# Attention, gated unit and soft mixture on one core: another spread of conversion and gated unit over the first eight pairs, and work of VectorE given to GpSimd and ScalarE

## The chip, the cores and the metric

One core of a Trainium2 chip runs the whole program. Times are device microseconds of one execution. The kernel before was run three times; its profile comes from one more execution.

## The reference

Three stages follow each other (numpy, shortened). The inputs q, k and phi are scaled by 8, so the exponentials are sharp.

```
# q, k, v: [4, 8, 1152, 64]
q_pool = q.reshape(B, H, S // 2, 2, D).mean(axis=3)          # 576 queries
scores = scale * q_pool @ k.T ; scores -= max(scores)
attn = exp(scores) / (sum + 1e-9) ; x = attn @ v               # -> [2304, 512]
g = x @ w_gate ; val = x @ w_val                               # [512, 1536] each
x = (g * sigmoid(g) * val) @ w_out                             # [1536, 512]
logits = x @ phi                                               # 32 slots
d = softmax of logits over the tokens ; slot_input = d.T @ x
slot_out[e] = relu(slot_input[e] @ w1[e]) @ w2[e]              # 8 experts
out = softmax of logits over the slots @ slot_out
```

## The kernel before, in words

The 32 heads are worked in 16 pairs (`steps`: batch b, pair p of 4). A pair has 21 units: nine of 128 keys by 512 queries for each of its two heads, and three that hold the remaining 64 queries of both. Operands are split into a high and a low half of 16 bits. A unit (`unit`, line 405) is two score matmuls into a bank (`st`), one exponential on ScalarE into P32 (line 419), and the difference P32 - PH (line 426) that gives the low half PL; PH is the upper 16 bits of P32 in place. The product with the values (`pv`, lines 457 to 459) follows three units later (LAG); P32 and PL have six buffers each (PB).

`DVE_PART` gives, for each pair, the share of the differences that VectorE does; GpSimd does the others, and a pair beyond the list has share 0. `F32_PART` gives the share of units that have no difference at all, because they multiply P32 itself with the values (lines 449 and 455).

`split_pair` (line 210) prepares the next pair while this one runs: it adds the two pooled queries (227), casts keys and queries (`kh`, `qh`, lines 230 and 232), takes their low halves (`ql` on VectorE, `kl` on GpSimd) and has SP's queue copy the halves to where the matmuls read them (lines 241 to 250). `cast` (line 179) puts a cast on ScalarE if its letter is in CASTS and the pair is one of the first eight, else on VectorE. `row_max` (line 315) finds the maxima of the next pair from kh and QD: 18 matmuls of 512 columns and nine of 128, each reduced on VectorE (329, 338); the maxima are joined (nm, 341), negated on ScalarE (mt, 310) and sent by a DMA from ScalarE's queue into row 64 of QH (347), for which the second score matmul (414) of every unit waits. The first pair's maxima (`row_max_first`) come from its own halves.

Weights are converted while pairs run. `prep` holds 36 items, for each of six slices of the gated unit two of `prep_wo` (613) and four of `prep_w` (647). Each loads 512 words a partition through SP's queue, has ScalarE work on both halves (600, 601) and VectorE join them (603). `prep_wo` then writes w_out's rows to HBM and multiplies them with phi on TensorE; `prep_w` casts on ScalarE (653) and takes the low half (655) on GpSimd, or on VectorE for three of the 24. Items come evenly from step PREP_BEG to step PREP_END (line 979). At the end of them three pieces of w_out are loaded.

The gated unit works in nine blocks of 256 tokens, each in six slices of 48 matmuls of 256 columns (`block_slice`, 671; its tanh is line 696). `moe_stream` (924) yields after every quarter of a slice, 31 times a block; a slice waits until its weights are converted, a block until its batch of four pairs is done. The loop at line 975 takes quanta from the stream so that from step 4 to step 16 the count grows evenly to 6.1 blocks. What is left runs after the last pair, then come the experts and the output.

Each engine's own order of instructions is planned by a scheduler from the order of the program, priorities and a timeline of its own; on the chip each engine then runs its list in order.

Of the kernel before, what the change touches and what calls it, by code (L numbers as in the profile page):

```python
# [29 lines left out]
HI_DVE, LO_PART = 0.0, 1.0  # L30
LD0, LDP = 1, 4
Y5E = 2
DVE_PART = [0.3, 0.3, 0.0, 0.3, 0.0, 0.3]
CAST_STEPS = 8
LO_DVE = 3
BAR = 2
# [9 lines left out]
MOE_LEAD = 6  # L46
PB, LAG = 6, 3
MOE_START = 4
N_MOE = 6.1
PREP_BEG, PREP_END = 1, 7  # L50
F32_PART = [0.17, 0.0, 0.17, 0.25, 0.33]
VRB = 2
HNB = 1
SUBS = ""
CASTS = "vqwxt"
OB = 4
AHEAD = 0
TXD = 1
# [6 lines left out]
def tile_pool_attention_glu_softmoe(  # L65
# [35 lines left out]
    def ps(tag, shape, dtype=F32, bufs=1, name=None):  # L101
        return psum.tile(shape, dtype, tag=tag, bufs=bufs, name=name or tag)
# [50 lines left out]
    steps = [(b, p) for b in range(B) for p in range(NP)]  # L153
# [14 lines left out]
    def load_pair(b, p):  # L168

        r = slice(D if (b, p) == steps[0] else 0, P)  # L170
        kr = at.tile([P, S], F32, tag="kraw", bufs=1, name=f"kr{b}_{p}")
        nc.sync.dma_start(out=kr[r], in_=kT[b, p, r])
        qr = at.tile([P, 2, SQ], F32, tag="qraw", bufs=1, name=f"qr{b}_{p}")
        nc.sync.dma_start(out=qr[r], in_=qT[b, p, r])
        vr = at.tile([P, 2, NCH, D + 1], F32, tag="vraw", bufs=VRB, name=f"vr{b}_{p}")
        nc.sync.dma_start(out=vr, in_=vP[b, p])
        raw[b, p] = (kr, qr, vr)

    def cast(what, b, p, dst, src):

        if b * NP + p < CAST_STEPS and what in CASTS:
            ins = nc.scalar.copy(dst, src)
# [174 lines left out]
    def later(n, fn):  # L357

        due.append((now[0] + n, fn))

    def tick(n=1):
        now[0] += n
        while True:
            run = [d for d in due if d[0] <= now[0]]
            if not run:
                return
            due.remove(run[0])
            run[0][1]()
# [18 lines left out]
    def maxima(n):  # L387
        while n_rm[0] < min(n, MX0 + MXP * (len(steps) - 1)):
            next(maxs)
            n_rm[0] += 1  # L390
# [3 lines left out]
    def of_step(parts, i):  # L394
        return parts[i] if i < len(parts) else 0.0

    def share(n, part):

        n[0] += part
        if n[0] >= 1.0:  # L400
            n[0] -= 1.0
            return True
        return False

    def unit(b, p, key, parts, n):
# [18 lines left out]
        PL = at.tile([P, QT], F16, tag="PL", bufs=PB, name=f"PL{b}_{p}_{key}")  # L424
        eng = nc.vector if share(n_dve, of_step(DVE_PART, b * NP + p)) else nc.gpsimd
        eng.tensor_tensor(out=PL[:, :o], in0=P32[:, :o], in1=PH[:, :o], op=ALU.subtract)  # L426
# [452 lines left out]
    def load(n, mark=None):  # L879
        key = order[n]  # L880
        ts = place(n, "_".join(map(str, key)))
        m = NQ // len(ts)

        piece[key] = [ts[e // m][:, e % m] for e in range(NQ)]
        for i, t in enumerate(ts):
            if key[0] == "w2":
                _, z, g, c = key
                k = HALF // ZW[z]
                t = t.rearrange("p e (c d) -> p e c d", c=k)
                for e in range(m):  # L890
                    src = w2[NQ * g + i * m + e, c * P:(c + k) * P, Z0[z]:Z0[z] + ZW[z]]
                    dma = nc.sync.dma_start(out=t[:, e], in_=src.rearrange("(c p) d -> p c d", p=P))
                    if mark and e >= Y5E:
                        after(dma, mark)
                continue
            if key[0] == "wo":
                src = wo_d[key[1] * NQ * P:(key[1] + 1) * NQ * P, :].rearrange("(c p) d -> p c d", p=P)
            else:
                e = slice(NQ * key[1] + i * m, NQ * key[1] + (i + 1) * m)
                src = w1[e, key[3] * P:(key[3] + 1) * P, key[2] * HALF:(key[2] + 1) * HALF]  # L900
                src = src.rearrange("e p f -> p e f")
            dma = nc.sync.dma_start(out=t, in_=src)
            if mark:
                after(dma, mark)
# [51 lines left out]
    moe_work = moe_stream()  # L956
    UNITS = 2 * (2 * NCH + 3)
    QPB = 5 * (NF // 2) + 1
    n_moe = QPB * N_MOE / (len(steps) - MOE_START)
    n_done = 0  # L960
    for i, (b, p) in enumerate(steps):
        for u, _ in enumerate(attn(b, p)):
            tick()
            f = (u + 1) / UNITS
            if u == (SPLIT0 if i == 0 else 0):
                if i + 1 < len(steps):
                    split_pair(*steps[i + 1])
                if i + 2 < len(steps):
                    later(0 if i == 0 else LOAD_LAG, lambda k=i + 2: load_pair(*steps[k]))

            if i:
                maxima(MX0 + MXP * i + int(MXP * min(1.0, max(0.0, f - MX_BEG) / (MX_END - MX_BEG))))
            else:
                maxima(9 + int((MX0 - 9) * min(1.0, f / MX0_END)) + int(MXP * min(1.0, max(0.0, f - MX1_BEG) / (MX1_END - MX1_BEG))))
            while i >= MOE_START and n_done < (i + f - MOE_START) * n_moe:
                if not next(moe_work, False):
                    break
                n_done += 1
            while prep and n_prep - len(prep) < (i + f - PREP_BEG) * n_prep / (PREP_END - PREP_BEG):
                prep.pop(0)()  # L980
                if not prep:
                    for n in range(NEE):
                        load(n)
# [25 lines left out]
    t = ps("st", [P, NF // 2, 2, NS], bufs=STB, name="gt")  # L1009
# [7 lines left out]
    t = ps("mm", [P, DM], bufs=MMB, name="si4p")  # L1017
# [11 lines left out]
    t = ps("tr", [P, ND, NS], bufs=TRB, name="siTp")  # L1029
# [44 lines left out]
    for g in range(E // NQ):  # L1074
        for h in range(2):
            t = ps("st", [P, HALF], bufs=STB, name=f"hp{g}_{h}")
# [9 lines left out]
            t = ps("mm", [P, NQ, P], bufs=MMB, name=f"hTp{g}_{h}")  # L1086
# [119 lines left out]
```

## Time and profile before

| | us |
|---|---|
| median of 3 runs | 917.54 (913.38 to 921.64) |
| profiled execution | 913.91 |
| its span | 912.1 |
| TensorE matmul busy | 823.9 (90%) |
| VectorE busy | 579.6 (64%) |
| GpSimd busy | 444.5 (49%) |
| ScalarE busy | 357.5 (39%) |

The span is from the first to the last instruction; the execution's time has the launch around it. In the views PE is TensorE, DVE VectorE, ACT ScalarE, POOL GpSimd, and SP the queue that issues most DMAs. A busy time is a sum over the span, so it says nothing of one stage; the rows below are cut by pair. The first exponential of pair 0 starts at 22.8 us, of pair 1 at 68.0, of pair 2 at 103.4, of pair 3 at 134.7, of pair 4 at 172.3, of pair 5 at 219.5, of pair 6 at 263.7, of pair 7 at 296.0, of pair 8 at 372.5.

### The profile page before, as it was taken

Reading aid. Unit: us, or ns where it says so; the run is one execution under the profiler, and the core shown is the slowest. Engines: PE = TensorE matmul, PEld = TensorE weight load, DVE = VectorE, ACT = ScalarE, POOL = GpSimd, SP = SyncE. Lnnn points to the kernel's source line nnn. Section 1 sums busy time; section 2 is a strip of 40 time slices with the busy share of each in tenths; the row PEclk is TensorE's granted clock in tenths of the full one; section 3 lists DMA queues with packets and bytes.
Section 4 is the critical chain, followed back from the end, with each engine's and each line's share of the span. In section 5 each row is a group of like instructions: output and inputs, shape, how many; then the busy total and the mean of one; then the engine's idle time right before and its main releaser. Section 6 shows DMA issues by size and latency. Waiting matters only on the chain.

```text
span 912.1 us, 23728 instructions
## 1 busy us (share of the span) xinstructions
PE 823.9 (90%) x9954; PEld 582.6 (64%) x9954; DVE 579.6 (64%) x1083; ACT 357.5 (39%) x682; POOL 444.5 (49%) x384
## 2 busy tenths in 40 slices
PE   3869789899887899999999998989999999998897
PEld 1445466577655577676767675767677787676445
DVE  6878677764987356677867775786672454444313
ACT  2437576664756233332433334224333322112112
POOL 8646685736689422835765677257556400000100
PEclk9989799799999899999999999999999999999999
DMA  6558858665878612615262625142411199248999
GB/s 174 157 137 232 180 161 246 156 200 131 258 185 249 177 52 25 167 25 143 56 156 42 168 45 136 36 108 38 83 25 37 37 292 333 56 140 204 280 291 290
DMA packets 154267, 134.69 MB, mean 148 GB/s; under 512 B 83632, under 2 KB 123120, under 8 KB 154160
## 3 DMA queue, kind: packets, MB, share of 16 engines
q1 hardware_dynamic: 152000, 133.13, 55.5%
q8 instruction: 78, 1.28, 0.6%
q10 hardware_dynamic: 2160, 0.04, 0.1%
q14 instruction: 29, 0.24, 0.1%
HBM read 84.10 MB, written 7.86 MB: 101 GB/s over the span
## 4 chain that ended last, share of the span: by engine, by line
PE 68%; DVE 16%; DMA 10%; issue 2%; ACT 2%; SPq 1%; POOL 0%; DVEq 0%; ACTq 0%; POOLq 0%
PE st L414 6%; PE st L413 6%; PE mx L323 5%; PE g L685 5%; PE v L685 5%; PE g L689 5%; PE g L690 4%; PE v L690 4%; PE v L689 4%; DMA QH<-mt 4%; DVE mp L329 3%; PE pv L457 3%; PE pv L458 3%; PE pv L459 3%; PE hp L1079 2%
## 5 line engine op out<-in xcount | busy, mean ns | idle before, releaser
L426 POOL TENSOR_TENSOR PL<-P 128x512 f16<-128x512 f32 (+1 forms) x295 | 323.1, 1108 | 234.6 <-ACT P L419 231.3
L419 ACT ACTIVATE P<-st 128x512 f32<-128x512 f32 (+1 forms) x336 | 189.8, 581 | 237.2 <-PE st L414 179.0
L329 DVE TENSOR_REDUCE mp<-mx 128x1 f32<-128x512 f32 x270 | 179.2, 683 | 58.3 <-PE mx L323 57.1
L414 PE MATMUL st<-QH,KL 65*128 65x512 f16 (+1 forms) x576 | 148.3, 296 | 9.8 <-DMA QH<-mt 9.4
L413 PE MATMUL st<-QQ,KK 128*128 128x512 f16 (+1 forms) x576 | 147.7, 293 | 6.8 <-ACT P L419 6.6
L457 PE MATMUL pv<-VV,P 128*128 128x65 f16 x1088 | 141.5, 194 | 1.1 <-DVE x L489 1.0
L458 PE MATMUL pv<-VV,P 128*128 128x64 f16 x1088 | 140.8, 196 | 0.0
L459 PE MATMUL pv<-VV,PL 128*128 128x65 f16 x1088 | 138.1, 193 | 3.0 <-DVE PL L426 2.7
L685 PE MATMUL g<-xT,wgv 128*128 128x256 f16 x432 | 120.1, 278 | 9.0 <-DVE hs L697 7.5
L323 PE MATMUL mx<-kh,QD 128*128 128x512 f16 x270 | 106.5, 414 | 22.0 <-DVE mp L329 12.7
L457 PEld LDWEIGHTS <-P 128*128 128x128 bf16 x1088 | 105.0, 99 | 24.5 <-issue 4.3
L689 PE MATMUL g<-xT,wgv 128*128 128x256 f16 x432 | 120.1, 278 | 0.0
L690 PE MATMUL g<-xT,wgv 128*128 128x256 f16 x432 | 120.0, 278 | 0.0
L685 PE MATMUL v<-xT,wgv 128*128 128x256 f16 x432 | 118.8, 275 | 0.2 <-DVE hs L697 0.2
L689 PE MATMUL v<-xT,wgv 128*128 128x256 f16 x432 | 118.5, 274 | 0.0
L690 PE MATMUL v<-xT,wgv 128*128 128x256 f16 x432 | 118.5, 274 | 0.0
L459 PEld LDWEIGHTS <-PL 128*128 128x128 f16 x1088 | 104.6, 100 | 19.1 <-DVE PL L426 3.5
L458 PEld LDWEIGHTS <-P 128*128 128x128 bf16 x1088 | 104.1, 99 | 12.0 <-issue 1.0
L685 PEld LDWEIGHTS <-wgv 128*128 128x128 f16 x864 | 86.0, 100 | 29.5 <-issue 6.9
L689 PEld LDWEIGHTS <-wgv 128*128 128x128 f16 x864 | 85.4, 99 | 21.6 <-issue 7.1
L690 PEld LDWEIGHTS <-wgv 128*128 128x128 f16 x864 | 85.5, 99 | 18.0 <-issue 0.8
L414 PEld LDWEIGHTS <-KL 65*128 65x128 f16 x576 | 52.8, 99 | 37.5 <-issue 23.2
(177 smaller groups left out, 1224.6 us busy)
## 6 DMA issues: line engine op xcount, KB each, us to landing
w<-in_w SPq DMA_DIRECT2D x16, 1024.0 KB, 7.6
w<-in_w SPq DMA_DIRECT2D x64, 256.0 KB, 5.4
vr<-in_vP SPq DMA_DIRECT2D x16, 585.0 KB, 6.2
KK<-kh SPq DMA_DIRECT2D x62, 144.0 KB, 3.3
qr<-in_qT SPq DMA_DIRECT2D x15, 576.0 KB, 5.8
kr<-in_kT SPq DMA_DIRECT2D x15, 576.0 KB, 4.7
r<-in_w_out SPq DMA_DIRECT2D x12, 512.0 KB, 4.1
r<-in_w_gate SPq DMA_DIRECT2D x24, 256.0 KB, 4.9
```

The lines of the kernel that those rows point to most:

```text
L323: nc.tensor.matmul(t, q, kh[:, k0:k0 + kw], start=True, stop=True)
L329: nc.vector.reduce_max(out=mp[:, g, c:c + 1], in_=t, axis=AX.X)
L413: nc.tensor.matmul(t[:, o:o + w], KK[:, k], QQ[:, q0:q0 + w], start=True, stop=False)
L414: nc.tensor.matmul(t[:, o:o + w], KL[:, k], QH[:, q0:q0 + w], start=False, stop=True)
L419: marks.append(nc.scalar.activation(P32[:, :o], t[:, :o], AF.Exp, scale=1.0 / 16.0).ins.name)
L426: eng.tensor_tensor(out=PL[:, :o], in0=P32[:, :o], in1=PH[:, :o], op=ALU.subtract)
L457: nc.tensor.matmul(dst[:, :D + 1], PH[:, q], VV[:, c, 0, :], start=first, stop=False, skip_group_check=True)
L458: nc.tensor.matmul(dst[:, :D], PH[:, q], VV[:, c, 1, :D], start=False, stop=False, skip_group_check=True)
L459: nc.tensor.matmul(dst[:, :D + 1], PL[:, q], VV[:, c, 0, :], start=False, stop=(c == NCH - 1), skip_group_check=True)
L685: mm = nc.tensor.matmul(o, w[:, 0, d, f], xh, start=(d == 0), stop=False)
L689: nc.tensor.matmul(o, w[:, 0, d, f], xl, start=False, stop=False)
L690: nc.tensor.matmul(o, w[:, 1, d, f], xh, start=False, stop=(d == ND - 1))
```

## The change

Four settings change, and the gated unit's pace becomes a line with a bend: 0 blocks at step 4, 1.0 at step 8, 6.1 at step 16. The conversion runs from step 2 to step 8. In pairs 0, 1 and 3 the differences of line 426 all go to GpSimd (pair 5 keeps its share of 0.3 on VectorE). The casts of the keys go to ScalarE in the first eight pairs, the first pair's half-cast among them.

```diff
-DVE_PART = [0.3, 0.3, 0.0, 0.3, 0.0, 0.3]
+DVE_PART = [0.0, 0.0, 0.0, 0.0, 0.0, 0.3]
...
-N_MOE = 6.1
-PREP_BEG, PREP_END = 1, 7
+
+MOE_PACE = [(4, 0.0), (8, 1.0), (16, 6.1)]
+PREP_BEG, PREP_END = 2, 8
...
-CASTS = "vqwxt"
+CASTS = "kvqwxt"
...
-    n_moe = QPB * N_MOE / (len(steps) - MOE_START)
+
+    def moe_due(t):
+        for (t0, m0), (t1, m1) in zip(MOE_PACE, MOE_PACE[1:]):
+            if t < t1:
+                return QPB * (m0 + (m1 - m0) * (t - t0) / (t1 - t0))
+        return QPB * MOE_PACE[-1][1]
+
...
-            while i >= MOE_START and n_done < (i + f - MOE_START) * n_moe:
+            while i >= MOE_START and n_done < moe_due(i + f):
```

## Rows read from the trace of the kernel before

**Rows 1.** Windows, pairs 0 to 7: stretch, length, busy us (instructions) by engine, clock, DMA.

```profile
22.80:68.00 45.20, 32.33 (x383) 20.32 (x382) 37.78 (x58) 17.61 (x33) 25.08 (x17) 0.89 0.53 147
68.00:103.40 35.40, 28.69 (x403) 18.11 (x402) 30.04 (x52) 23.67 (x46) 22.47 (x18) 0.89 0.69 183
103.40:134.70 31.30, 28.63 (x339) 19.33 (x337) 21.53 (x39) 23.44 (x47) 24.36 (x22) 0.88 0.79 202
134.70:172.30 37.60, 33.21 (x411) 22.15 (x411) 29.20 (x49) 24.44 (x47) 24.81 (x19) 0.86 0.73 195
172.30:219.50 47.20, 45.90 (x487) 35.03 (x485) 29.25 (x51) 27.72 (x53) 24.47 (x21) 0.95 0.60 166
219.50:263.70 44.20, 39.30 (x559) 27.87 (x557) 35.47 (x62) 27.31 (x52) 29.77 (x22) 1.00 0.74 211
263.70:296.00 32.30, 26.15 (x344) 17.43 (x342) 26.81 (x40) 22.38 (x45) 30.63 (x26) 0.96 0.91 252
296.00:372.50 76.50, 72.76 (x863) 53.83 (x861) 42.16 (x81) 21.84 (x42) 29.86 (x26) 0.95 0.37 88
```

The engines stand in the order PE, PEld (weight loads), DVE, ACT, POOL.

**Rows 2.** Chain of waits, 0 to 70 us: start, length, what.

```profile
7.87 2.75 DVE kh L184
...
26.47 0.58 DVE kh L184
...
32.51 2.10 DVE PL L426
...
45.00 0.81 DVE PL L426
...
49.10 1.09 DVE PL L426
...
62.66 0.67 DVE kh L184
...
63.70 3.61 DMA QH<-mt
```

**Rows 3.** Groups of VectorE's instructions in pair 1 (68.0 to 103.4 us).

```profile
L603 DVE SCALAR_TENSOR_TENSOR r<-r 128x512 uint32<-128x512 uint32 x6 | 6.1, 1022 | 1.1 <-ACT r L601 1.1
L426 DVE TENSOR_TENSOR PL<-P 128x512 f16<-128x512 f32 (+1 forms) x6 | 4.6, 765 | 0.7 <-POOL PL L426 0.7
```

A group has its line, engine, operation, output and input, count, then busy us, mean ns of one, idle us before them and what ended it.

**Rows 4.** Chain of waits in pair 3 (134.7 to 172.3 us).

```profile
148.93 5.00 DMA r<-in_w_val
```

**Rows 5.** GpSimd's groups by form over the span, and VectorE's timeline near 26 us.

```profile
L426 POOL TENSOR_TENSOR PL<-P 128x512 f16<-128x512 f32 x254 | 286.9, 1142 | 211.1 <-ACT P L419 208.0 <-PE pv L458 1.6 <-POOL PL L426 0.3
L252 POOL TENSOR_TENSOR VV<-vr,VV 128x1152 f16<-128x1152 f32 x16 | 39.4, 2460 | 14.6 <-ACT VV L182 10.2 <-DVE rs L487 4.3
L236 POOL TENSOR_TENSOR kl<-kr,kh 128x1152 f16<-128x1152 f32 x15 | 38.1, 2537 | 17.3 <-DVE kh L184 11.0 <-DMA QH<-qh 3.6 <-DVE rs L487 1.5
L426 POOL TENSOR_TENSOR PL<-P 128x384 f16<-128x384 f32 x41 | 36.4, 896 | 23.5 <-ACT P L419 23.2
...
25.85 0.70 DVE L426 TENSOR_TENSOR PL<-P 128x512 f16<-128x512 f32 x1
```

**Rows 6.** ScalarE's groups by form over the span: the values' cast.

```profile
L182 ACT CAST VV<-vr 128x1170 f16<-128x1170 f32 x8 | 9.5, 1190 | 3.4 <-PE pv L449 2.2 <-DMA vr<-in_vP 1.2
```

**Rows 7.** Windows with the tanh alone, one for each slice: pairs 6, 7, 12, 13.

```profile
263.70:296.00 32.30, 0.00 (x0) 0.96 0.91 252
296.00:372.50 76.50, 4.16 (x7) 0.95 0.37 88
...
548.10:604.20 56.10, 2.95 (x5) 0.97 0.37 92
604.20:642.30 38.10, 0.59 (x1) 0.96 0.33 63
```

**Rows 8.** Windows around the steps to pair 1 and to pair 5.

```profile
61.50:71.50 10.00, 5.46 (x21) 2.05 (x20) 5.86 (x12) 2.95 (x6) 5.26 (x4) 0.51 0.70 158
...
215.00:223.00 8.00, 7.11 (x119) 5.84 (x116) 2.25 (x3) 5.62 (x10) 5.47 (x6) 1.00 0.92 222
```

## The prediction, written before the changed kernel was run

> **What bounds the kernel now.** I first cut the span at the first exponential of each pair of heads and read the busy times of each stretch [rows 1]. Over the pairs TensorE is nearly full wherever gated-unit work fills it: 45.90 of 47.20 us in pair 4, 72.76 of 76.50 in pair 7. In the pairs without such work it is not: 32.33 of 45.20 in pair 0, 28.69 of 35.40 in pair 1, 33.21 of 37.60 in pair 3. What ends last there is seen in the second view, the chain of waits. In the start-up and pair 0 it runs mostly on VectorE: casts of the keys, maxima, and differences P - PH (the low half of an exponential) are links of it [rows 2]. In pair 1 VectorE is busy 30.04 of 35.40 us, 6.1 of them in the conversion's join and 4.6 in six differences [rows 1, 3]. Pair 2, which already has no difference on VectorE, has a chain of matmuls and is the shortest, 31.30 us [rows 1]. Pair 3 is longer, but a part of it is a 5.00 us wait of ScalarE for a conversion's load [rows 4], which the change does not remove. So VectorE's work in pairs 0, 1 and 3 is on the path; GpSimd's and ScalarE's there are not (25.08 and 17.61 of 45.20 us in pair 0).
>
> **The change part by part**, against the profiled execution's span of 912.1 us (its time is 913.91 us, 3.6 below the median of the runs, 917.54; I apply the difference to the median).
>
> *Keys' cast, start-up.* The first half-cast of 2.75 us lies on VectorE's unbroken chain from 7.87 us to the first maxima [rows 2]. ScalarE would do it in about the 1.19 us of its cast of the values, nearly the same shape [rows 6], in time in which it has nothing: its next cast of the queries waits for VectorE. What is late next is the rest of that same VectorE chain. Between 0 (the load of the queries arrives too late to use the gap) and -2.75 us; I take -2.7.
>
> *Pair 0.* The part up to the second head's maxima has on the chain a keys' cast (0.58 us after 0.49 of waiting and 0.93 of issue around it) and a difference of 2.10 us, which ran beside GpSimd's own work; another difference took 0.70 us undisturbed [rows 2, 5]. I take -4.0, from -1 (only part is not refilled) to -4.5. Later two differences (0.81 and 1.09 us), a cast of 0.67 us and a conversion step go: -2.5, from 0 to -4. The five differences of this pair go to GpSimd at 1.14 us each [rows 5], 5.7 us beside 25.08 busy of 45.20: covered. If that cover were gone the P V matmuls, three units behind, would wait for them.
>
> *Pair 1.* The six differences go (4.6 us), and the whole conversion moves to pair 7 (6.1 us of joins; its loads and the write to HBM on SP's queue, its activations and copies on ScalarE, its transposes on TensorE go with it) [rows 3]. With 10.7 us of VectorE gone TensorE and GpSimd are next. GpSimd then holds 21 differences, at 1.14 us for the full ones and 0.90 for the three short ones [rows 5], with about 5.0 us for the low halves of keys and values: 28.2 us, below the length of pair 2. So I take pairs 2 and 6 (31.3 and 32.3 us) as the new length: -3.5, from 0 to -5.
>
> Here a rule speaks against the change. GpSimd's undisturbed price stands to VectorE's as 1.14 to 0.70 [rows 5], 1.6 times. The Trainium skill (GPSIMD Engine Reference, section Engine selection) keeps two-input elementwise work on VectorE because GpSimd is about 2 times slower. At twice 0.70 us GpSimd would hold about 33 us in pair 1, the pair would not fall below that, and 1 to 1.5 us of the gain would go. The rows decide for the smaller price.
>
> *Pair 3.* Five differences, about 4 us at pair 1's mean price, leave VectorE, but the load wait of 5.00 us [rows 4] stays. -2.5, from 0 to -5.
>
> *Pair 7 takes the conversion in.* There TensorE is full [rows 1], so its few transposes and products count fully, and the joins delay in part: +3, from 0 (hidden, as in pair 2) to +6 (all joins of pair 1).
>
> *Keys' cast in pairs 1 to 7.* On VectorE it stood ahead of the last reduction of the maxima (0.67 us, then the 3.61 us transfer of the maxima into QH, with TensorE empty [rows 2]). On ScalarE's in-order queue it may stand ahead of the negation that feeds this transfer, and behind it the next exponentials, whose bank st the score matmuls wait for; SP's copies of the keys follow it as before, some 0.5 us later. Seven times between -0.67 and +1.19 [rows 2, 6]: -4.7 to +8.3. ScalarE is idle at those points (23.44 busy of 31.30 us even in pair 2), and the nearest row, the values' cast with 3.4 us of waiting in eight, says small: +1.
>
> *Pace of the gated unit.* Counted out from the loops, 12 slices are issued in pairs 4 to 7 now and 6 after; six go to pairs 8 to 15, and 6.1 blocks stand at the end either way, so the tail is unchanged. The work is the same; only its price differs. Early it is (76.5 - 32.3)/7 = 6.3 us a slice, late (56.1 - 38.1)/4 = 4.5 [rows 7]. That would give six times -1.8 = -11. Against it stands cover: TensorE's empty time in pairs 4 to 7 is 1.3 + 4.9 + 6.2 + 3.7 = 16.1 us, and would be 24.6 if each became like pair 6, which has no slice: +8.5. Each pair keeps one or two slices, so I take 0.
>
> Sum: -2.7 - 4.0 - 2.5 - 3.5 - 2.5 + 3 + 1 + 0 = -11.2 us: a span of 901, a median of 906.3.
>
> **The rivals.**
> 1. *The late price holds.* Slices cost 4.5 us in pairs 8 to 15, where nothing else needs the gaps; half of the -11 comes on top of the sum: about 900. For it: pair 13, with one slice, still has 38.1 us, 6 more than pair 6. Against: pair 7's price holds a block's end too.
> 2. *The relieved time is taken back.* The differences on GpSimd lengthen VectorE's two-input work beside them (0.70 us alone, 2.10 beside GpSimd [rows 2, 5]), ScalarE's casts come before the maxima's negation, and a conversion load such as that of 5.00 us is waited for once more. Start-up and pair 0's first part stay (-6.7), the rest of the relief (-8.5) is lost; with +3, +1 and nothing for the slices that is -2.7: 915.
> 3. *Slower: empty boundaries between pairs 4 and 8.* Where no slice covers the step from one pair to the next, TensorE runs empty and the granted clock falls: around the step to pair 1 it is 0.51, that is the lower level of 1.2 GHz, with 5.46 us busy of 10; around the step to pair 5 the clock stays 1.00 and 7.11 of 8 are busy [rows 8]. The first costs 4.5 us empty and 2.7 of slowness, 7.2; the second 0.9. The Trainium skill (TensorE: Matmul & The Clock Gate, section What's actually happening) calls the throttled state the default and activity what lifts it; the trace agrees in these two rows. Thinning the slices could make the steps to pairs 5 to 8 like the first, 6.3 us each: with three of them +18.9 on -11.2, +7.7: 925, and up to 932 if the relief is also halved. It decides from two such steps on (12.6 against 11.2). Against it: by the code one slice is released just before the steps to pairs 6, 7 and 8, as the last weights come in.
> 4. *The new pace is not reached*, since slices also wait for converted weights: the first block's last slice then starts at 7.95 instead of 6.95 whatever the pace says. That moves the burst from pair 7 to pair 8 without changing its size; it gives the forecast's time and has no chance of its own.
>
> **How the numbers follow.** Forecast 0.45 (its own range 897 to 914, two thirds of it under 908.4), rival 1 0.20, rival 2 0.20, rival 3 0.15. What a measurement of this kernel can tell from no change is about 1%, 9 us. Faster by over 1%: 0.30 + 0.20 = 0.50. Within 1%: 0.15 + 0.18 + 0.03 = 0.36. Slower: 0.02 + 0.12 = 0.14. The predicted time is the forecast's, 906. The range reaches down past rival 1 to 892 and up to 922, over rival 2 and the milder part of rival 3.
>
> **What would show it.** The first exponential at about 20 instead of 22.8 us shows the start-up term. Pair 0 near 38.5 us, pair 1 near 32, pair 3 near 35 show the relief; VectorE under 22 us busy in pair 1. Chain pieces of L426 on GpSimd in pairs 0 to 3 speak for rival 2, as does the keys' cast on ScalarE between the last reduction and the transfer to QH. Granted clocks near 0.5 at the steps between pairs 4 and 8 speak for rival 3. Pairs 8 to 15 longer by 27 us say the late price, by 38 the early one. I would be wrong if the span up to pair 4 falls by less than 5 us, or if pairs 4 to 15 together grow by more than 10.

## The result and the profile after

The changed kernel takes 890.59 us (median of 4 runs, 887.54 to 893.72) against 916.59 of the kernel before on the same chip: a ratio of 0.9708, 95% interval 0.9665 to 0.9751. The forecast was 906 and the range ended at 892. The profiled execution's span is 885.8 us, 26.3 below the one before; it is the shortest of the four runs, 3 us under their median.

The windows of pairs 0 to 7 in the changed kernel, with the columns of [rows 1]; the last two rows hold pairs 8 to 15 and pairs 4 to 15 in one:

```profile
22.80:61.30 38.50, 32.15 (x383) 20.10 (x382) 28.80 (x50) 18.80 (x33) 28.43 (x22) 0.95 0.58 157
61.30:86.00 24.70, 22.58 (x311) 14.88 (x310) 17.28 (x29) 15.07 (x29) 23.69 (x22) 0.94 0.49 122
86.00:121.50 35.50, 30.19 (x395) 20.55 (x394) 30.17 (x49) 24.44 (x46) 25.02 (x21) 0.90 0.63 190
121.50:157.70 36.20, 33.22 (x382) 22.71 (x381) 26.64 (x43) 26.26 (x50) 27.47 (x23) 0.86 0.73 203
157.70:201.20 43.50, 40.98 (x485) 31.46 (x484) 24.38 (x44) 27.32 (x52) 23.64 (x21) 0.92 0.61 185
201.20:239.50 38.30, 34.30 (x479) 23.99 (x477) 34.66 (x56) 26.87 (x52) 28.12 (x22) 1.00 0.73 210
239.50:274.70 35.20, 32.97 (x466) 23.04 (x465) 29.52 (x50) 24.90 (x48) 31.68 (x27) 1.00 0.81 224
274.70:309.90 35.20, 30.37 (x404) 21.02 (x404) 29.33 (x48) 23.00 (x46) 33.71 (x25) 1.00 0.81 251
309.90:692.90 383.00, 378.13 (x4798) 279.78 (x4798) 246.42 (x473) 136.28 (x258) 213.01 (x185) 1.00 0.36 81
157.70:692.90 535.20, 516.75 (x6623) 379.29 (x6622) 364.30 (x669) 238.37 (x454) 330.16 (x277) 0.99 0.47 119
```

and the same stretch, pairs 4 to 15, in the kernel before:

```profile
172.30:719.80 547.50, 518.84 (x6563) 377.49 (x6562) 370.48 (x663) 225.92 (x431) 326.60 (x273) 0.98 0.44 110
```

Pair 4 starts at 157.7 instead of 172.3 us: 14.6 us come from before it, 12.3 from pairs 4 to 15, and the tail behind 692.9 us is 0.6 longer. Pair 1's 24.7 us look better than they are, since its window holds 311 matmuls against 403 [rows 1]; pairs 1 to 3 together went from 104.3 to 96.4. In pairs 4 to 15 TensorE's empty time (length less PE busy) fell from 28.7 to 18.4 us, and the granted clock rose from 0.98 to 0.99.

The same cut through most of the kernels that ran orders what follows; the letter and number name the run, which is told below. "Up to pair 4" is when pair 4's first exponential starts. "Empty" is the time in pairs 4 to 15 in which TensorE has no matmul. "Low clock" is the time there at the lower of its two clock levels, 1.2 instead of 2.4 GHz; in pair 4 of the changed kernel, which has all of it, the clock column gives it as 2 x (1 - 0.92) x 43.50 = 7 us. "Rest" is the length of pairs 4 to 15 less the empty time and half of the time at the low clock. Each row is of one profiled execution, in us:

| kernel | up to pair 4 | pairs 4 to 15 | empty | low clock | rest |
|---|---|---|---|---|---|
| before | 172.3 | 547.5 | 28.7 | 21.9 | 507.8 |
| changed | 157.7 | 535.2 | 18.4 | 6.8 | 513.3 |
| a1_pace_only | 170.6 | 534.1 | 16.6 | 17.5 | 508.7 |
| a2_diffs_keycast | 162.4 | 559.7 | 32.6 | 41.0 | 506.7 |
| x1_even_pace | 161.1 | 567.7 | 38.7 | 41.0 | 508.5 |
| x2_old_conv | 162.9 | 537.1 | 19.7 | 13.7 | 510.6 |
| x3_old_diffs | 164.3 | 536.6 | 22.4 | 0.0 | 514.1 |
| x4_old_keycast | 158.8 | 546.7 | 21.8 | 27.3 | 511.3 |
| p1_gap12 | 156.5 | 540.7 | 25.2 | 10.2 | 510.4 |
| p2_burst7 | 155.9 | 558.7 | 35.2 | 30.7 | 508.1 |
| e1_early_weights | 172.5 | 534.9 | 20.2 | 20.5 | 504.5 |
| e2_lumps | 159.8 | 542.4 | 29.3 | 10.2 | 508.0 |
| e4_pace06 | 159.2 | 544.5 | 25.9 | 20.5 | 508.4 |
| h1_keycast_to_4 | 156.4 | 546.1 | 22.5 | 23.9 | 511.6 |

The rest moves by 10 us while the stretch moves by 34. So most of what a setting is worth behind pair 4 stands in the two columns before it. The half is only a first guess: a straight-line fit over all 20 traces gives 1.07 us of stretch for each us empty and 0.30 for each us at the low clock.

One execution is not the kernel. Two kernels were profiled twice. The changed one (again in r1) reached pair 4 at 157.7 and 157.8 us and took 535.2 and 537.7 us for pairs 4 to 15, with 18.4 and 18.9 empty and 6.8 and 10.2 at the low clock. The kernel of e3 (again in r2) took 536.7 and 541.6, with 19.5 and 24.9 empty and 6.8 and 3.4 at the low clock. Kernels that differ from the changed one in the pace alone, which acts from pair 4 on, reach pair 4 anywhere from 155.9 to 161.1. So differences of some 5 us between two rows show nothing by themselves. Some profiled executions also lie off their kernel's median: those of x1 and a2 are 5.8 and 5.2 us above it, those of a1 and x4 6.1 and 4.9 below.

### The profile page after: what moved, and what is told of

It reads as the page before. It is cut to its first block, busy times and chain, and to the rows that moved or that the text cites. A ratio compares the mean times of both kernels' runs of the same rounds, so it can differ in the third digit from the quotient of the medians.

```text
span 885.8 us, 23743 instructions
## 1 busy us (share of the span) xinstructions
PE 820.3 (93%) x9954; PEld 584.9 (66%) x9954; DVE 558.3 (63%) x1059; ACT 366.1 (41%) x690; POOL 455.7 (51%) x400
## 4 chain that ended last, share of the span: by engine, by line
PE 70%; DVE 13%; DMA 9%; issue 3%; POOL 2%; ACT 2%; SPq 1%; DVEq 0%; ACTq 0%; POOLq 0%
PE st L415 6%; PE st L414 6%; PE g L686 5%; PE v L686 5%; PE mx L324 5%; PE v L691 5%; PE g L691 5%; PE v L690 5%; PE g L690 5%; DMA qr<-in_qT 3%; PE pv L458 3%; DVE mp L330 3%; PE pv L459 3%; PE pv L460 3%; PE pv L450 2%
## 5 line engine op out<-in xcount | busy, mean ns | idle before, releaser
L427 POOL TENSOR_TENSOR PL<-P 128x512 f16<-128x512 f32 (+1 forms) x311 | 337.1, 1097 | 213.4 <-ACT P L420 208.9
L686 PE MATMUL g<-xT,wgv 128*128 128x256 f16 x432 | 118.6, 274 | 3.4 <-DVE hs L698 3.1
L691 PE MATMUL g<-xT,wgv 128*128 128x256 f16 x432 | 118.5, 274 | 0.0
L690 PE MATMUL g<-xT,wgv 128*128 128x256 f16 x432 | 118.4, 274 | 0.0
L324 PE MATMUL mx<-kh,QD 128*128 128x512 f16 x270 | 103.7, 404 | 10.1 <-DVE mp L330 5.5
L415 PEld LDWEIGHTS <-KL 65*128 65x128 f16 x576 | 51.6, 98 | 33.9 <-issue 13.4
```

Source lines behind the costliest of these rows:

```text
L324: nc.tensor.matmul(t, q, kh[:, k0:k0 + kw], start=True, stop=True)
L415: nc.tensor.matmul(t[:, o:o + w], KL[:, k], QH[:, q0:q0 + w], start=False, stop=True)
L686: mm = nc.tensor.matmul(o, w[:, 0, d, f], xh, start=(d == 0), stop=False)
L690: nc.tensor.matmul(o, w[:, 0, d, f], xl, start=False, stop=False)
L691: nc.tensor.matmul(o, w[:, 1, d, f], xh, start=False, stop=(d == ND - 1))
```

## The experiments

All ratios are against the kernel before, run beside it on the same chip, with the 95% interval in brackets. The runs are spread over several chips, on which the kernel before took 912.81 to 918.05 us, so kernels are compared by their ratios; 0.01 is 9 us. The changed kernel itself was run once more, on another chip (r1 below), and had 0.9741 there instead of 0.9708, so a loss against it carries some 3 us of doubt. Line numbers in the rows are one higher than before, as the change added a line.

**One part undone.** Each kernel is the changed one with one setting put back.

```diff
# x1_even_pace
-MOE_PACE = [(4, 0.0), (8, 1.0), (16, 6.1)]
+MOE_PACE = [(4, 0.0), (16, 6.1)]
# x2_old_conv
-PREP_BEG, PREP_END = 2, 8
+PREP_BEG, PREP_END = 1, 7
# x3_old_diffs
-DVE_PART = [0.0, 0.0, 0.0, 0.0, 0.0, 0.3]
+DVE_PART = [0.3, 0.3, 0.0, 0.3, 0.0, 0.3]
# x4_old_keycast
-CASTS = "kvqwxt"
+CASTS = "vqwxt"
```

> The changed kernel with the old even pace of the gated unit (0 at step 4 to 6.1 blocks at step 16); conversion, differences and keys' casts stay changed. By the loops pairs 4 to 11 then issue 3, 1, 1, 7, 4, 3, 3, 2 slices, and no slice is at hand from 7.95 to 8.24 and from 11.81 to 12.24. Theory A (the gain behind pair 4 comes from the pace: slices at hand at every step between pairs, so TensorE is neither empty nor slow there): the time up to pair 4 stays at 158 us, and 10 to 14 us of the 26 are lost: 901 to 905, with empty time and half-clock stretches back around the steps to pairs 8, 9, 12 and 13. Rival B (the pace only moves work at an equal price, the gain behind pair 4 is the later conversion): within 4 us of the changed kernel, 887 to 895.

Measured 918.27 us, ratio 1.0016 [0.9992, 1.0040]: with the old pace the three other parts are worth nothing. Pairs 7 and 8 of this kernel:

```profile
283.40:330.60 47.20, 36.54 (x440) 24.54 (x439) 26.80 (x44) 23.20 (x46) 35.13 (x30) 0.82 0.73 209
330.60:435.40 104.80, 98.96 (x1120) 74.00 (x1118) 60.70 (x121) 27.45 (x55) 29.58 (x24) 0.97 0.31 70
```

with the slices in them, counted by their tanh:

```profile
283.40:330.60 47.20, 0.57 (x1) 0.82 0.73 209
330.60:435.40 104.80, 7.11 (x12) 0.97 0.31 70
```

Pair 7 has one slice: TensorE is empty for 10.7 us and its mean clock is 0.82. Then twelve slices come in pair 8. Theory A has the direction, but its loss of 10 to 14 us was too small against 28; B is refuted.

> The changed kernel with the conversion from step 1 to 7 as before; pace, differences and keys' casts stay changed. Theory A: pair 1 takes the six joins back (some 5 us), pair 7 gives them up (3 us): 890 to 895. Rival B (the later conversion is what gained): 9 us or more slower, 900 or above.

891.81 us, 0.9709 [0.9678, 0.9739]: as the changed kernel. The shift of the conversion is worth nothing beside the new pace; beside the old one it costs some 9 us, as a2 against x1 shows below.

> The changed kernel with VectorE's old share of the differences in pairs 0, 1 and 3. Theory A (VectorE is the bound in pair 0 and shares it in 1 and 3): pair 0 back by 5 us, pairs 1 and 3 by 2 each: 896 to 901. Rival B (the relief of VectorE is taken back by GpSimd anyway): within 3 us of the changed kernel.

898.36 us, 0.9790 [0.9739, 0.9842]. Theory A: in the profile 6.6 us of the 14.6 before pair 4 go, 1.4 behind.

> The changed kernel with the keys' casts on VectorE again. Theory A: the start-up does not change (first exponential at 22.8 us in both traces), and each pair of the first eight loses up to 0.7 us: 891 to 896. Rival B: the cast on ScalarE delays its exponentials by as much: 886 to 891.

904.75 us, 0.9850 [0.9814, 0.9887]: 10 to 14 us lost, more than either said. In the profile only 1.1 us are lost before pair 4 and 11.5 behind it, with 3.4 us more of empty time and 20.5 more at the low clock. The slices also lie otherwise, though the pace is the same: pairs 4 to 7 have 2, 2, 0 and 1 of them, against 2, 1, 1 and 1 in the changed kernel. That alone does not bring the low clock, since x3 has 2, 2, 0 and 1 as well and no low clock at all in pairs 4 to 15.

**One part or two alone**, on the kernel before: a1 has the new pace only, a2 the differences and the keys' casts only.

> The kernel before with the new pace alone (1.0 block at step 8, 6.1 at 16); conversion, differences and keys' casts are the old ones. Theory A (the pace keeps a backlog, so slices are at hand at the steps to pairs 8, 9, 12 and 13): the stretch up to pair 4 stays at 172 us, pairs 4 to 15 lose 12 us or more: 899 to 905. Rival B (the pace gains only because the relief ahead of it left something to fill): 912 to 918.

906.29 us, 0.9877 [0.9830, 0.9923]. A little above A's range, far from B's. Its pairs 4 to 15 in one, to be held against the two rows above:

```profile
170.60:704.70 534.10, 517.54 (x6556) 378.09 (x6555) 359.04 (x664) 225.99 (x431) 321.51 (x272) 0.98 0.45 112
```

The stretch is 13.4 us shorter than before, with TensorE empty for 16.6 us instead of 28.7. The execution is a short one; by the medians the kernel gains 11 us.

> The kernel before with the differences and the keys' casts of the changed one; pace and conversion are the old ones. Theory A (two gains that add up): up to pair 4 about 12 us less, pairs 4 to 15 as before: 902 to 907. Rival B (what the relief brings up to pair 4 is given back behind it when the gated unit waits for weights and batches): 912 to 919.

910.72 us, 0.9922 [0.9889, 0.9954]: between the two ranges, since a part of the relief is given back. In the profile 9.9 us are won before pair 4 and 12.2 lost behind it, but this execution is 5.2 us above the median; by the medians 6 to 7 us of the 9.9 are kept. Pairs 6 and 7 of a2:

```profile
260.90:295.50 34.60, 26.87 (x351) 18.01 (x350) 23.00 (x36) 21.71 (x45) 31.06 (x26) 0.89 0.84 247
295.50:368.50 73.00, 70.87 (x850) 52.44 (x849) 43.27 (x82) 21.67 (x42) 28.39 (x24) 0.98 0.35 84
```

Pair 6 is empty for 7.7 us at a mean clock of 0.89, pair 7 holds the pile, as [rows 1, 7] show for the kernel before (no slice in pair 6, seven in pair 7). The two parts bring 0.9922 x 0.9877 = 0.980 if they multiply; with both (x2) it is 0.9709, some 8 us better. They need each other. The reading that fits the rows, though no run singles it out, is that attention that gets ahead earlier only waits if there is no slice to fill it. The later conversion makes the old pace worse (1.0016 in x1 against 0.9922 in a2); in x1 the last weights come one pair later, and the pile lies in pair 8 instead of pair 7.

**What in the pace counts.** p1 and p2 are the changed kernel with other bends.

```diff
-MOE_PACE = [(4, 0.0), (8, 1.0), (16, 6.1)]
# p1_gap12
+MOE_PACE = [(4, 0.0), (8, 1.0), (12, 4.0), (16, 6.1)]
# p2_burst7
+MOE_PACE = [(4, 0.0), (8, 2.0), (12, 3.2), (16, 6.1)]
```

> The changed kernel with a pace of 1.0 block at step 8, 4.0 at step 12, 6.1 at step 16. By the loops 2, 2, 1, 1 slices in pairs 4 to 7 and the step to pair 8 are as in the changed kernel, but the fourth block ends at 11.98 and the fifth begins at 12.24, so that no slice is at hand at the step to pair 12. Theory A (slices at hand at the steps between pairs): empty time and half clock come back in pairs 11 to 13, 4 to 9 us: 895 to 900. Rival C (how many slices lie in pairs 4 to 7 decides): 888 to 893, as the changed kernel.

893.19 us, 0.9739 [0.9718, 0.9760]: 2.6 us slower than the changed kernel's first runs and level with its second (0.9741 in r1). No loss is shown, and the time is at the edge of C's range. Around the step to pair 12, from 524 to 534 us, TensorE was 10.00 of 10 us busy at a clock of 1.00: no slice released there leaves no gap there. Theory A, as a rule on single steps, falls.

> The changed kernel with a pace of 2.0 blocks at step 8, 3.2 at 12, 6.1 at 16. By the loops slices of the first two blocks pile up behind the weights (seven are issued at 7.95 at once) and no slice is at hand from 7.95 to 8.24; at the step to pair 12 there is one. Theory A: pairs 7 and 8 lose as with the even pace (there 104.8 + 47.2 us against 58.2 + 35.2, with six more slices issued in them), pairs 12 and 13 do not: 905 to 915. Rival D (the whole unevenness behind pair 8 costs, not the pile): 890 to 898.

907.54 us, 0.9894 [0.9856, 0.9931], in A's range: 17 us lost by asking for two blocks at step 8 when the weights allow fewer. Pair 7 again has 10.1 us empty and 16.7 us at the low clock, and pair 8 a pile of ten slices.

The next two separate the pile from the number of slices: e1 keeps the old pace and lets no slice wait for weights; e2 keeps the new one and releases three slices at once.

```diff
# e1_early_weights
-MOE_PACE = [(4, 0.0), (8, 1.0), (16, 6.1)]
-PREP_BEG, PREP_END = 2, 8
+MOE_PACE = [(4, 0.0), (16, 6.1)]
+PREP_BEG, PREP_END = 1, 5.5
# e2_lumps
-            while i >= MOE_START and n_done < moe_due(i + f):
+            while i >= MOE_START and n_done < (moe_due(i + f) if i < 9 else 15 * (moe_due(i + f) // 15)):
```

> The changed kernel with the old even pace, but the conversion from step 1 to 5.5, so that no slice waits for weights: by the loops 4, 3, 3, 2 slices in pairs 4 to 7 and no pile at 6.95 or 7.95. As many slices as in the old kernel before pair 8 (12), and still no slice at hand from 7.88 to 8.24 and 11.81 to 12.24. Theory E (what costs is the pile: slices released at once run on TensorE one after the other at about 6.1 us each with no attention between, and single slices cost 4.5): no run of 48 or more gated-unit matmuls, 893 to 904 even with the denser conversion. Rival A (the steps to pairs 8 and 12 without a slice cost) or C (the number of slices before pair 8 decides): 908 to 918.

904.84 us, 0.9862 [0.9814, 0.9910], just above E's range, and the split says more than the sum: the denser conversion costs 14.8 us before pair 4 (172.5 against 157.7), and pairs 4 to 15 take 534.9 us, as in the changed kernel, with the old pace. a2, which differs in the conversion alone, takes 559.7. Pairs 4 to 7 of e1, with the slices:

```profile
172.50:224.30 51.80, 1.79 (x3) 0.87 0.64 191
224.30:273.50 49.20, 1.76 (x3) 1.00 0.76 196
273.50:319.50 46.00, 2.36 (x4) 1.00 0.44 104
319.50:361.40 41.90, 1.18 (x2) 1.00 0.50 106
```

Twelve slices before pair 8 are not dearer than five, if they do not wait: against the changed kernel pairs 4 to 7 are 36.7 us longer with seven slices more, and pairs 8 to 15 are 37.0 us shorter with seven fewer, 5.2 and 5.3 us a slice. That speaks against C (the number early decides) and the rest of A. It is not a clean test: by the loop e1 has twelve of the 36 conversion items behind pair 4, the changed kernel 24. x2 has 18 of them there and is not shorter for it (537.1 us), but e1's low rest (504.5) may come from there.

> The changed kernel, but from pair 9 on the quanta of the gated unit are released fifteen (three slices) at a time instead of one by one; the amount per stretch is the same. Theory E: some 27 slices go from 4.5 to near 6.1 us where the three run one behind the other: 15 to 45 us slower, 905 to 935, all of it behind pair 9, with the exponentials' longest gaps back at 12 to 20 us. Rival F (the scheduler spreads a lump by itself, the price is from elsewhere): 888 to 896.

899.27 us, 0.9808 [0.9764, 0.9852]: slower, as E says, but below its range. Runs of 48 or more of the gated unit's matmuls without one of attention between hold 396 matmuls here and 48 in the changed kernel, about seven slices more; pairs 9 to 15 are 7.3 us longer, 1 us for each piled slice and not 1.6. TensorE's empty time in these pairs went from 2.0 to 12.4 us, more than the whole loss. So the loss goes with the gaps between the piles; that the pile itself costs is not seen.

```diff
# e4_pace06
-MOE_PACE = [(4, 0.0), (8, 1.0), (16, 6.1)]
+MOE_PACE = [(4, 0.0), (8, 0.6), (16, 6.1)]
```

> The changed kernel with 0.6 instead of 1.0 block asked at step 8 (6.1 at 16 as before). By the loops 1, 1, 1, 1 slices in pairs 4 to 7, no slice waits for its weights, 4 or 5 in each pair behind. Theory E: the one small pile at 7.95 (a run of 48 matmuls in the changed kernel) is gone, the rest as it is: 886 to 892. Rival C (fewer slices early is better, each moved one gains 1.6 us): 883 to 887. Rival I (pairs 4 to 7 now have empty time that nothing fills): 893 to 900.

899.25 us, 0.9815 [0.9762, 0.9868]: in rival I's range. Too little early leaves gaps too: 25.9 us empty, 7.5 more than in the changed kernel, and 20.5 at the low clock. But only 2.0 of the 7.5 lie in pairs 4 to 7, where I puts them.

**The start-up.** The identity's cast goes to ScalarE:

```diff
-    nc.vector.tensor_copy(out=id16, in_=id32)
+    nc.scalar.copy(id16, id32)
```

> The changed kernel with the cast of the identity (2.37 us on VectorE's chain in the start-up, beside GpSimd's two differences) on ScalarE. Theory G (VectorE's work in the start-up is stretched by what GpSimd runs beside it, 7.3 to 11.2 us, so what leaves the chain is partly made up by longer work behind it): the first exponential comes 0 to 1.5 us earlier, the sum of the pooled queries is again near 1.85 us or longer: 888 to 892. Rival H (the chain simply gets shorter by the cast): first exponential near 20.4 us, 886 to 888.

886.51 us, 0.9671 [0.9616, 0.9725], and the first exponential at 19.56 us instead of 22.84: 3.3 us, more than H's 2.4. VectorE's timeline in the start-up of the changed kernel:

```profile
7.54 2.37 DVE L108 CAST id<-id 128x128 f16<-128x128 f32 x1
9.95 1.85 DVE L228 TENSOR_TENSOR qr<-qr 64x576 f32<-64x576 f32 x1
11.82 2.48 DVE L285 TENSOR_REDUCE mp<-mx 128x1 f32<-128x512 f32 x4
14.34 2.71 DVE L235 TENSOR_TENSOR ql<-qr,qh 64x576 f16<-64x576 f32 x1
```

GpSimd's beside it:

```profile
7.30 2.53 POOL L209 TENSOR_TENSOR KL<-wgv,KK 64x1152 f16<-64x1152 f32 x1
9.91 1.27 POOL L208 TENSOR_TENSOR QQ<-wgv,QQ 64x576 f16<-64x576 f32 x1
...
14.07 2.36 POOL L237 TENSOR_TENSOR kl<-kr,kh 64x1152 f16<-64x1152 f32 x1
```

and VectorE's in e3:

```profile
9.07 1.41 DVE L228 TENSOR_TENSOR qr<-qr 64x576 f32<-64x576 f32 x1 [1.43 <-DMA qr<-in_qT]
10.51 2.48 DVE L285 TENSOR_REDUCE mp<-mx 128x1 f32<-128x512 f32 x4
13.02 0.76 DVE L235 TENSOR_TENSOR ql<-qr,qh 64x576 f16<-64x576 f32 x1
```

Of the 2.37 us of the cast only 0.9 are won, because VectorE now waits 1.43 us for the load of the queries. The rest of the 3.3 us comes from behind it: the sum of the queries takes 1.41 instead of 1.85 us, and their low half 0.76 instead of 2.71, as it now runs before GpSimd's kl, which starts at 14.61 us in e3, and not beside it. So G is right that what leaves the chain changes the lengths of the work behind it, but wrong in the sign: here they became shorter.

To see whether the 3.3 us reach the end, both kernels ran side by side:

> The changed kernel again, beside the next one on one chip: 888 to 893.

> The changed kernel with the identity's cast on ScalarE, again: if the 3.2 us of the start-up reach the end, 3 to 5 us below the changed kernel beside it; if not, within 1.5 us of it.

890.45 us (0.9741 [0.9701, 0.9781]) and 888.25 us (0.9694 [0.9654, 0.9734]). e3's kernel is ahead by 2.2 us here, and by 4.1 us against the changed kernel's first runs on another chip, but the intervals overlap both times: likely, not settled.

**The keys' casts and the rest.** h1 has them on VectorE for pairs 4 to 7 alone. The f kernels start from e3's: f1 with the old conversion and 1.3 blocks at step 8, f2 with no difference on VectorE at all, f3 with the keys' casts on ScalarE in all pairs.

```diff
# h1_keycast_to_4
-        if b * NP + p < CAST_STEPS and what in CASTS:
+        if b * NP + p < (4 if what == "k" else CAST_STEPS) and what in CASTS:
# f1_id_pace13
-PREP_BEG, PREP_END = 2, 8
+PREP_BEG, PREP_END = 1, 7
-MOE_PACE = [(4, 0.0), (8, 1.0), (16, 6.1)]
+MOE_PACE = [(4, 0.0), (8, 1.3), (16, 6.1)]
# f2_id_nodiffs
-DVE_PART = [0.0, 0.0, 0.0, 0.0, 0.0, 0.3]
+DVE_PART = []
# f3_id_keycast_all
-        if b * NP + p < CAST_STEPS and what in CASTS:
+        if (b * NP + p < CAST_STEPS or what == "k") and what in CASTS:
```

> The changed kernel with the keys' casts on ScalarE only for pairs 0 to 3, on VectorE again for pairs 4 to 7. With all eight on VectorE 14 us were lost, 1 of them before pair 4 and 12 behind it, of which 10 are low clock around the steps to pairs 6 to 8. Theory J (a cast and whatever slips in with it ahead of the last reduction of the maxima lengthens the step between pairs, TensorE runs empty there and its clock falls): 899 to 905, the half-clock stretches behind pair 4 back at 15 us or more against 6.8. Rival K (the loss comes from the first four pairs, whose order shifts everything behind): 888 to 893.

896.04 us, 0.9815 [0.9787, 0.9844]. In us it lies between J and K, but the kernel before took only 912.81 us beside it. By the ratios h1 loses 7 to 10 us against the changed kernel, where x4 loses 10 to 13: most of the loss belongs to the casts of pairs 4 to 7, as J says. Its pairs 4 to 15 take 546.1 us, as with all eight casts on VectorE (546.7), with 23.9 us at the low clock.

How a cast of 0.75 us brings that about is not shown. h1's pairs 4 to 7 hold 2, 2, 0 and 1 slices, as in x4. Around the step to pair 7 of x4 a join of the conversion (1.65 us at 272.09) and a key cast stand on VectorE ahead of the join of the maxima, and TensorE waits 3.0 us for the transfer of the maxima into QH. The changed kernel has the same cast at that place (1.19 us at 268.46, the cast of pair 8's keys, which is on VectorE in both), but the conversion's join behind, and TensorE waits 1.0 us. That is J's mechanism at one step, not the undone casts themselves.

> The changed kernel with the identity's cast on ScalarE, the old conversion (steps 1 to 7) and 1.3 blocks asked at step 8: by the loops two slices in each of pairs 4 to 7, only one short wait for weights, 2 to 4 in the pairs behind. Theory E (no pair starved of slices and no pile): pairs 4 to 15 and the tail at 532 to 538 us, in all 884 to 890. Rival L (more slices before pair 8 meet the conversion on VectorE and ScalarE): 891 to 898.

892.19 us, 0.9777 [0.9739, 0.9815]: in rival L's range, and by the ratios 8 to 10 us behind e3's kernel. Pairs 4 to 15 take 535.1 us, which is no longer than in e3, but it takes 160.0 us up to pair 4 against e3's 153.2, with the conversion back in pair 1. The slices came as 2, 3, 0 and 4, not two in each pair, so the evenly filled pairs that E asks for were not reached.

> The changed kernel with the identity's cast on ScalarE and no difference on VectorE in pair 5 either. Pair 5 has VectorE 34.6 us busy of 38.3: relieving it gives 2 to 4 us if it is the bound there, 883 to 886; GpSimd, at 31.7 of 35.2 us in pair 6, gives it back if its backlog grows: 887 to 892.

899.91 us (891.60 to 904.23), 0.9872 [0.9827, 0.9917]: slower than e3, and more so than the second theory said. In the profile, which is the shortest of the four runs and 8 us under their median, pair 5 takes 39.3 us against e3's 37.9 with GpSimd 33.9 instead of 28.8 us busy, and pair 7 becomes 44.9 us with GpSimd 35.4 busy. That fits GpSimd taking the relief back.

> The changed kernel with the identity's cast on ScalarE and the keys' casts on ScalarE in all sixteen pairs. Behind pair 8 TensorE is empty for 5 us in all and never slow, so a shorter step between pairs finds nothing to shorten: within 2 us of the kernel with the identity's cast alone, 884 to 889. Rival: the cast on ScalarE holds up the gated unit's tanh, 890 to 896.

889.73 us, 0.9745 [0.9716, 0.9774]: between the two ranges, and no gain over e3's kernel (0.9671 and, in r2, 0.9694).

## Why the prediction was wrong

*Up to pair 4 it held as a sum, and partly by luck.* Predicted -15.2 us, measured -14.6. Pair 0: -6.5 predicted, -6.7 measured. Pairs 1 to 3: -6.0 predicted, -7.9 measured. The start-up's -2.7 was 0.0: the 2.75 us cast left VectorE's chain, and the identity's cast went from 1.18 to 2.37 us, the sum of the queries from 0.76 to 1.85, their low half from 1.84 to 2.71, each beside GpSimd's differences. The prediction named the lengthening, but only for rival 2 and only for the differences. It also called the difference of 0.70 us [rows 5] undisturbed; that one ran while GpSimd did four differences, from 23.47 to 28.96 us, so such work is not always lengthened.

*The miss lies behind pair 4.* There the sum has +4 us (the conversion's +3, the keys' casts' +1, the pace's 0), and pairs 4 to 15 became 12.3 us shorter. None of the signs that the prediction gave for being wrong came: the span up to pair 4 fell by more than 5 us, and pairs 4 to 15 did not grow.

*The conversion* was put at +3 in pair 7. Its whole shift, with what it saves in pair 1, is worth -1 to 0 beside the new pace (x2).

*The keys' casts* were put at +1 in pairs 1 to 7, with a low end of -4.7, and -2.7 in the start-up. Together they are worth -10 to -14 beside the new pace (x4), 7 to 10 of them from pairs 4 to 7 (h1), outside the range. A step of the chain was priced at its own length; what showed instead is 14 to 21 us more at the low clock in pairs 4 to 15 when the casts are on VectorE (h1, x4). Why a cast does that stays open.

*The step that failed is the pace of the gated unit*, taken at 0 between -11 and +8.5. Alone it is worth -11 us (a1), beside the other three -25 to -28 (x1 against the changed kernel). The values of single parts do not add up to the change's 26 us, since the parts need each other. Three arguments under the 0 were wrong.

The first was the cover, +8.5, which set off the cheaper late slices: with fewer slices pairs 4 to 7 would all become like pair 6, and TensorE's empty time there would go from 16.1 to 24.6 us. It fell to 13.6, with seven slices fewer. The old pace asked for slices whose weights were not there: pair 6 got none, and seven came in pair 7 [rows 7]. The new one gives 2, 1, 1 and 1.

The second was that an early slice costs 6.3 us and a late one 4.5. Pairs 8 to 15 became 35.7 us longer with seven slices more, 5.1 each, between the late price and the early one, and e1 gives 5.2 early and 5.3 late. So the early slices seem to have looked dear because they waited and piled up, and not because they were early.

The third was rival 4's sentence that the burst only moves to pair 8. It was counted for the weights alone; with less asked for, little has piled up when they come (one run of 48 matmuls in pairs 4 to 15 of the changed kernel, three with 168 before). Rival 1's time, 900, was nearest, for the wrong reason: the late price did not hold.

*Rival 2* (the relief taken back) has its like under the old pace: a2 gives a part of the relief back behind pair 4. But there it is empty time and low clock, not the lengthened work and the waits that the rival names. Its sign, chain pieces of the differences on GpSimd, came in pair 0 (3.5 us) and not in pairs 1 to 3. *Rival 3's* mechanism, empty time and low clock where slices are missing, is seen in x1 (pair 7, one slice) and a2 (pair 6, none), and the change runs it backwards: low clock in pairs 4 to 15 went from 21.9 to 6.8 us, 10.2 in the second profile.

The rule that rival 3 cites from the Trainium skill (TensorE: Matmul & The Clock Gate, section What's actually happening), that activity lifts the throttle, agrees with the table in kind: the two kernels with the most low clock, 41.0 us, have 32.6 and 38.7 us of empty time. It is no strict order: x3 is empty for 22.4 us and never at the low clock there.

The rule of the Trainium skill (GPSIMD Engine Reference, section Engine selection) that GpSimd is about 2 times slower in two-input work did not decide: GpSimd did the 21 differences of pair 1 in 21.39 us and was busy 23.69 us in its window, which the values' low half falls outside of, and not the 33 worked out from the rule.

## What to carry to other kernels

Filler work is worth what it fills: count when each piece can start (its weights, its batch), since a pace that asks for pieces that are not ready starves some stages and piles up in the next. A relief ahead of such a stage can show up as waiting behind it until the pace is mended: here three of the four parts are worth nothing beside the old pace (x1), and all four are worth 3%. So try parts together as well as one by one, and compare ratios, not times from different chips. Price a stall of TensorE with the low clock that comes with it, and cut the span where the stages change: empty time and time at the low clock showed where the stretch had grown, which busy times over the whole span do not. Profile a kernel twice before reading a difference of 5 us.

## What the runs showed of the hardware

Work of VectorE with both operands in SBUF, and its casts, took up to 3.6 times as long beside GpSimd's two-input work (0.76 us in e3 and 2.71 in the changed kernel for 64x576; 1.18 before and 2.37 in the changed kernel for the identity's cast, both beside GpSimd, 0.29 on ScalarE). It is not so each time: four full differences that ran wholly beside such work before took 0.70 to 2.18 us, seven clear of it 0.68 to 0.69. Reductions of 128x512 from PSUM were untouched: 0.68 us on average in the 152 of the changed kernel that ran wholly beside GpSimd's two-input work, and 0.68 in the 65 clear of it.

With the keys' casts on VectorE in pairs 4 to 7, casts of some 0.75 us, pairs 4 to 15 ran 23.9 and 27.3 us at the lower clock level (h1, x4) against 6.8 and 10.2 in the two profiles of the changed kernel. That the casts cause it step by step is not shown; e4 and f1, with these casts on ScalarE, have 20.5.
